# Column maximum of k in three two-input steps, one subtraction for a pair of heads, and a rounding moved to ScalarE, in a fused linear attention and two-MLP kernel

## The chip, the cores and the metric

The kernel runs on one core of one Trainium2 chip. The metric is the device time of one execution in microseconds (us), lower is better. The kernel before was timed in three runs: 1659.59, 1660.09 and 1670.22 us, with a median of 1660.09 us. One more execution was taken under the hardware profiler; all rows shown in this document come from such profiled executions.

## The reference

```python
q_s = softmax of q over its 64 features          # exp(q - max) / (sum + 1e-9)
k_s = softmax of k over its 576 positions        # exp(k - max over positions) / (sum + 1e-9)
kv  = einsum('bhsd,bhse->bhde', k_s, v)          # one 64x64 matrix for each batch and head
x   = einsum('bhsd,bhde->bhse', q_s, kv)         # 8 batches, 8 heads, 576 positions, 64 features
x   = x as 4608 tokens of 512 features
x   = relu(x @ w_in1)**2 @ w_out1                # 512 -> 2048 -> 512
out = silu(x @ w_in2) @ w_out2                   # 512 -> 2048 -> 512
```

All of it is in single precision; the four weight matrices arrive in double precision and are converted on the chip. The line that the change touches is the softmax of k: the maximum is taken for each of the 64 columns over all 576 positions.

## The kernel before, in words

**Stages.** The work is a stream of products on TensorE (PE) in blocks of 512 tokens. First the attention of batch 0 is computed, then the first MLP of block 0 while the attention of batch 1 is made. Blocks 1 to 8 of the first MLP follow, each in eight turns, one for each pair of 128-row slices of the hidden layer. A turn computes the hidden part with seven products in place of eight (`strassen`, its matmuls all on L602), applies the square of relu (`relu2`), and adds the products with the output weights of the turn before (`out_pair`, matmuls on L188 to L190 in `mm3`). Wherever precision needs it, a float32 value is split into a rounded part and a rest: `split` (L116 to L118) lets ScalarE (ACT) copy the value into a rounded type and VectorE (DVE) subtract that copy from the source. From about 705 us on, no attention is left, and from about 900 us on the second MLP runs.

**Attention.** Batches 1 to 7 are worked off in 28 pairs of heads by a generator, `attention()` (L445). It has four phases for each pair (`phase`, L427): the maxima of k and q and the exponent of q; the subtraction and exponent of k and the norm of q; the product of k and v with the transposition of q; the product with q and its evacuation. The main loop asks for one phase at two places of each turn (the `hook` calls with 1 and 6), so a pair lasts two turns; in two turns of block 1 a further phase is asked for, so the first pairs follow each other faster. Batches 0 and 1 are `natural` (`by_chunk = 2`): they keep k's columns as head, feature. In batches 2 to 7, with 24 pairs, the columns of the exponent tile `k` are stored as feature half, head, feature in the half.

**What the pair does with k.** `load` brings k as tile `kr`, 128 partitions by two heads by five chunks by 64 features. `k_max` (L267) reduces the five chunks to one row for each partition, tile `m`; POOL then takes the maximum over the partitions into `mb` (L279). `k_sub` (L283) subtracts `mb` into `k`, `k_exp` (L299) takes the exponent on ACT, and `kv` (L302) multiplies slices of 32 of its columns with v, including a column of ones which gives the sum. `kv_evac` (L313) divides by that sum and masks (L315, L316, L318, tile `m` again), and splits the result into `kvh` and `kvl`, both on DVE (L329, L330). `x` (L400) multiplies them with q. The tile `m` exists once, so the maxima of the next pair cannot be written there until the rounded parts have been read.

**Order.** Each engine executes its instructions in one fixed order. That order is worked out when the kernel is built, from the order of the code and from the build's own estimates of when each input is ready; it differs from the order of the code, except for instructions pinned by `keep_in_program_order`. All loads and stores are issued from one queue, SP, also in order.

Of the kernel before, what the change touches and what calls it, by code (L numbers as in the profile page):

```python
# [10 lines left out]
F32 = mybir.dt.float32  # L11
# [7 lines left out]
AX = mybir.AxisListType  # L19
PSUM = bass.MemoryType.PSUM  # L20
DRAM = bass.MemoryType.DRAM
P = 128
# [9 lines left out]
def kernel(  # L32
# [13 lines left out]
    nc = tc.nc  # L46
    B, H, S, D = q.shape
# [7 lines left out]
    SC = SM // P  # L55
# [36 lines left out]
    def f32(t):  # L92
        return t.bitcast(F32)
# [22 lines left out]
    def split(hi, lo, src):  # L116
        nc.scalar.copy(hi, src)  # L117
        nc.vector.tensor_sub(lo, src, f32(hi))  # L118
# [83 lines left out]
    class Pair:  # L202
# [63 lines left out]

        def k_max(self):  # L267
            m = self.tile("m", [P, 2, D], F32)
            if self.natural:
                t = self.tile("km", [P, 2, 2, D], F32)  # L270
                nc.vector.tensor_max(t, self.kr[:, :, 0:2], self.kr[:, :, 2:4])
                nc.vector.tensor_max(t[:, :, 0], t[:, :, 0], t[:, :, 1])
                r = nc.vector.tensor_max(m, t[:, :, 0], self.kr[:, :, 4])
            else:
                r = nc.vector.reduce_max(m, self.kr.rearrange("p a c d -> p a d c"), axis=AX.X)  # L275
            if (self.b, self.p) == (1, 0):
                tc.keep_in_program_order(r)
            self.m = self.tile("mb", [P, 2, D], F32)
            nc.gpsimd.partition_all_reduce(  # L279
                self.m.rearrange("p a d -> p (a d)"), m.rearrange("p a d -> p (a d)"), P, bass_isa.ReduceOp.max  # L280
            )

        def k_sub(self):  # L283
            self.k = self.tile("k", [P, SC + 1, 2 * D], F32)
            if self.natural:
                nc.vector.tensor_sub(
                    self.k.rearrange("p c (a d) -> p c a d", a=2),
                    self.kr.rearrange("p a c d -> p c a d"),
                    self.m.rearrange("p (c a) d -> p c a d", c=1).to_broadcast([P, SC + 1, 2, D]),
                )  # L290
                return
            for a in range(2):
                nc.vector.tensor_sub(
                    self.k.rearrange("p c (dh a dl) -> p c dh a dl", dh=2, a=2)[:, :, :, a],
                    self.kr[:, a].rearrange("p c (dh dl) -> p c dh dl", dh=2),
                    self.m[:, a].rearrange("p (c dh dl) -> p c dh dl", c=1, dh=2).to_broadcast([P, SC + 1, 2, 32]),
                )

        def k_exp(self):  # L299
            nc.scalar.activation(self.k, self.k, AF.Exp)  # L300
# [1 line left out]
        def kv(self):  # L302
            self.kvp = self.bank(self.p % 2, "kvp")
            n = D if self.natural else 32
            for c in range(SC + 1):
                for i in range(P // n):
                    r = slice(n * i, n * i + n)
                    nc.tensor.matmul(
                        self.kvp[r, 0:D + 1], self.k[:, c, r], self.v[:, c, i % 2],
                        start=(c == 0), stop=(c == SC), skip_group_check=True,  # L310
                    )

        def kv_evac(self):  # L313
            rec = self.tile("rec", [P, 1], F32)
            nc.vector.tensor_scalar_add(rec, self.kvp[:, D:D + 1], 1e-9)  # L315
            nc.vector.reciprocal(rec, rec)  # L316
            t = self.tile("m" if not self.early else "kvt", [P, 2 * D], F32)
            nc.vector.scalar_tensor_tensor(  # L318
                out=t.rearrange("p (a d) -> p a d", a=2),
                in0=self.kvp[:, 0:D].rearrange("p (a d) -> p a d", a=1).to_broadcast([P, 2, D]), scalar=rec,  # L320
                in1=(mask_n if self.natural else mask_t).rearrange("p (a d) -> p a d", a=2),
                op0=ALU.mult, op1=ALU.mult,
            )
            if self.natural:
                self.kv32 = t
                return
            self.kvh = self.tile("kvh", [P, 2 * D], F32R)
            self.kvl = self.tile("kvl", [P, 2 * D], F32R)
            nc.vector.tensor_copy(self.kvh, t)  # L329
            nc.vector.tensor_sub(self.kvl, t, f32(self.kvh))  # L330

        def swap(self, t, name):
            u = apool.tile([P, S32], F32, tag=name, name=name)
# [383 lines left out]
    for a in range(2):  # L717
        e = slice(D * a, D * a + D)
        nc.gpsimd.memset(mask_n[e, e], 1.0)
        for dh in range(2):  # L720
            r = 64 * dh + 32 * a
# [12 lines left out]
    for i in range(NK + 2):  # L734
        a = early[i] if i < NK else None
        b = early[i - 1] if 1 <= i <= NK else None
        c = early[i - 2] if 2 <= i else None
# [54 lines left out]
    t = 0  # L792
# [143 lines left out]
```

## Time and profile before

| quantity | value |
|---|---|
| median of three runs | 1660.09 us |
| profiled execution, its own time | 1662.81 us |
| its span, first to last instruction | 1661.0 us |
| PE busy | 1610.4 us, 97% |
| DVE busy | 996.2 us, 60% |
| ACT busy | 855.8 us, 52% |
| mean granted TensorE clock | 0.999 |
| first and last start of the maximum of k in batches 2 to 7 (L275) | 145.9 and 681.9 us |

The profile gives, for a group of equal instructions, the line, the engine, the operation, output and inputs with shapes, the count, the busy time in us with the mean in ns, and the idle time just before them with what ended it ("releaser"). A row of the waits reads: who waited, for whom, us in total, number of waits, the longest. A row of the timeline reads: start, duration, engine, line, operation. A window row reads: from and to, length, then busy us of PE, of PE's weight loads, of DVE, ACT and POOL. An engine that is idle without holding up another costs nothing.

### The profile page before, as it was taken

How to read it: one execution, taken by the hardware profiler on the slowest of the kernel's cores; microseconds unless marked ns; L12 is line 12 of the kernel's file. 1: busy time of each engine (PE TensorE's matmuls, PEld its weight loads, DVE VectorE, ACT ScalarE, POOL GpSimd, SP SyncE). 2: the span in 40 equal slices, each digit the busy share in tenths (PEclk: the TensorE clock that was granted, in tenths of full speed). 3: DMA queues.
4: the chain of work that ended last, by engine and by line, in shares of the span. 5: the costliest groups of instructions: out<-in, count | busy, mean ns of one | idle time of the engine just before them, and what ended most of it. 6: DMA issues, size and time to landing. Idle time of an engine off the chain costs nothing.

```text
span 1661.0 us, 24854 instructions
## 1 busy us (share of the span) xinstructions
PE 1610.4 (97%) x9624; PEld 1396.8 (84%) x9624; DVE 996.2 (60%) x1695; ACT 855.8 (52%) x1505; POOL 54.4 (3%) x150
## 2 busy tenths in 40 slices
PE   4999999999999999999999999999999999999999
PEld 3566888888888888889998889898988989999897
DVE  7999896886868687642436675345344344444333
ACT  4876675666666565654546554334334334334332
POOL 2000000000001000000000000000000000000000
PEclk9999999999999999999999999999999999999999
DMA  7776767678685776745346864543543543544621
GB/s 207 258 226 192 234 208 255 200 218 240 183 259 156 231 206 221 227 168 199 137 171 244 335 248 161 187 184 123 189 174 128 193 165 134 196 156 148 221 96 39
DMA packets 193510, 320.40 MB, mean 193 GB/s; under 512 B 113264, under 2 KB 142960, under 8 KB 188528
## 3 DMA queue, kind: packets, MB, share of 16 engines
q1 hardware_dynamic: 193392, 318.81, 57.6%
q8 instruction: 76, 1.25, 0.3%
q14 instruction: 42, 0.34, 0.1%
HBM read 248.51 MB, written 70.25 MB: 192 GB/s over the span
## 4 chain that ended last, share of the span: by engine, by line
PE 75%; DVE 10%; DMA 6%; ACT 5%; issue 2%; POOL 1%; SPq 0%; POOLq 0%; DVEq 0%; ACTq 0%
PE a L602 19%; PE c L602 14%; PE y L189 8%; PE y L190 8%; PE y L188 8%; PE op L189 5%; PE op L188 5%; PE op L190 5%; DMA raw<-in_moe_w_in_dram 3%; PE hp L655 2%; DMA raw<-in_moe_w_out_dram 2%; DVE g L118 1%; ACT raw L142 1%; DVE m L275 1%; DVE u L150 1%
## 5 line engine op out<-in xcount | busy, mean ns | idle before, releaser
L602 PE MATMUL a<-x,wah 128*128 128x256 f32 (+1 forms) x1792 | 397.7, 309 | 10.7 <-ACT h L636 6.4
L602 PEld LDWEIGHTS a<-x,wah 128*128 128x128 f32 x1792 | 313.4, 189 | 55.9 <-ACT h L636 11.7
L602 PE MATMUL c<-x,wah 128*128 128x256 f32 (+1 forms) x1344 | 293.4, 305 | 0.2 <-DVE h L623 0.2
L602 PE MATMUL a<-x,wal 128*128 128x256 f32 (+1 forms) x896 | 275.4, 307 | 0.0
L189 PE MATMUL op<-g,w 128*128 128x512 f32 x576 | 229.3, 398 | 3.1 <-DVE g L118 3.1
L188 PE MATMUL op<-g,w 128*128 128x512 f32 x576 | 229.2, 402 | 3.0 <-ACT g L117 3.0
L190 PE MATMUL y<-wb,g 128*128 128x512 f32 x576 | 227.8, 396 | 0.0
L189 PE MATMUL y<-wb,g 128*128 128x512 f32 x576 | 227.4, 395 | 0.0
L602 PEld LDWEIGHTS c<-x,wah 128*128 128x128 f32 x1344 | 225.0, 190 | 1.7 <-DVE h L623 0.6
L190 PE MATMUL op<-g,w 128*128 128x512 f32 x576 | 225.5, 391 | 0.0
L188 PE MATMUL y<-wb,g 128*128 128x512 f32 x576 | 223.2, 389 | 0.4 <-ACT wb L117 0.4
L602 PE MATMUL c<-x,wal 128*128 128x256 f32 (+1 forms) x672 | 204.8, 305 | 0.0
L872 ACT ACTIVATE z<-h 128x768 f32<-128x768 f32 x96 | 81.3, 847 | 226.9 <-DVE h L631 225.7
L602 PEld LDWEIGHTS a<-x,wal 128*128 128x128 f32 x896 | 168.9, 189 | 0.2
L623 DVE TENSOR_TENSOR h<-c,h 128x256 f32<-128x256 f32 (+1 forms) x112 | 53.7, 480 | 190.7 <-PE c L602 189.2
L644 ACT ACTIVATE h<-h 128x512 f32<-128x512 f32 x128 | 80.8, 632 | 105.1 <-DVE h L631 103.7
L118 DVE TENSOR_TENSOR g<-h,g 128x512 fp32r<-128x512 f32 x128 | 88.0, 688 | 77.7 <-ACT g L117 77.4
L118 DVE TENSOR_TENSOR g<-z,g 128x768 fp32r<-128x768 f32 x96 | 91.9, 957 | 67.3 <-ACT g L117 66.9
L627 DVE TENSOR_TENSOR h<-a,h 128x256 f32<-128x256 f32 (+1 forms) x112 | 53.5, 477 | 127.9 <-PE a L602 127.9
L620 ACT COPY h<-a 128x256 f32<-128x256 f32 (+1 forms) x112 | 47.1, 420 | 159.2 <-PE a L602 159.2
L190 PEld LDWEIGHTS op<-g,w 128*128 128x128 f32 x576 | 108.9, 189 | 23.7
L602 PEld LDWEIGHTS c<-x,wal 128*128 128x128 f32 x672 | 127.6, 190 | 0.0
(150 smaller groups left out, 2323.3 us busy)
## 6 DMA issues: line engine op xcount, KB each, us to landing
wah<-wad SPq DMA_DIRECT2D x72, 896.0 KB, 6.5
wal<-wad SPq DMA_DIRECT2D x72, 896.0 KB, 6.0
wb<-wbd SPq DMA_DIRECT2D x30, 1024.0 KB, 4.9
raw<-in_moe_w_in_dram SPq DMA_DIRECT2D x32, 512.0 KB, 5.3
raw<-in_moe_w_out_dram SPq DMA_DIRECT2D x32, 512.0 KB, 5.3
wad<-wah SPq DMA_DIRECT2D x16, 896.0 KB, 4.1
wad<-wal SPq DMA_DIRECT2D x16, 896.0 KB, 5.0
x1d<-o SPq DMA_DIRECT2D x18, 512.0 KB, 5.2
```

What stands on the lines that cost most here:

```text
L118: nc.vector.tensor_sub(lo, src, f32(hi))
L142: first = nc.scalar.activation(f32(lo32), lo32, AF.Copy, scale=2.0 ** -51, bias=2.0)
L188: nc.tensor.matmul(ps, lh, rh, start=first, stop=False)
L189: nc.tensor.matmul(ps, lh, rl, start=False, stop=False)
L190: nc.tensor.matmul(ps, ll, rh, start=False, stop=last)
L602: nc.tensor.matmul(ps, l, r, start=first and c == 0 and n == 0, stop=c == 1 and n == 2, skip_group_check=True)
L620: nc.scalar.copy(h[:, 0, two], a)
L623: nc.vector.tensor_add(h[:, 0, two], c, h[:, 0, two])
L627: nc.vector.tensor_add(h[:, 1, two], a, h[:, 1, two])
L644: nc.scalar.activation(h, src, AF.Relu)
L655: nc.tensor.matmul(hp, f32(w[:, s]), XR[0][:, c], start=c == 0, stop=c == NK - 1)
L872: nc.scalar.activation(z, h, AF.Sigmoid)
```

## The change

In batches 2 to 7 the maximum over the five chunks is no longer one reduction, but three maxima of two inputs, as batches 0 and 1 already have; the subtraction is one instruction for both heads instead of one for each, with k's columns in the order head, feature; the matmuls of `kv` pick their 32 columns from that order, and write the same rows; and the rounded part `kvh` is made by `split`, so by ACT instead of DVE. Batches 0 and 1 execute the same instructions as before.

```diff
         def k_max(self):
             m = self.tile("m", [P, 2, D], F32)
-            if self.natural:
-                t = self.tile("km", [P, 2, 2, D], F32)
-                nc.vector.tensor_max(t, self.kr[:, :, 0:2], self.kr[:, :, 2:4])
-                nc.vector.tensor_max(t[:, :, 0], t[:, :, 0], t[:, :, 1])
-                r = nc.vector.tensor_max(m, t[:, :, 0], self.kr[:, :, 4])
-            else:
-                r = nc.vector.reduce_max(m, self.kr.rearrange("p a c d -> p a d c"), axis=AX.X)
+            t = self.tile("km", [P, 2, 2, D], F32)
+            nc.vector.tensor_max(t, self.kr[:, :, 0:2], self.kr[:, :, 2:4])
+            nc.vector.tensor_max(t[:, :, 0], t[:, :, 0], t[:, :, 1])
+            r = nc.vector.tensor_max(m, t[:, :, 0], self.kr[:, :, 4])
...
         def k_sub(self):
             self.k = self.tile("k", [P, SC + 1, 2 * D], F32)
-            if self.natural:
-                nc.vector.tensor_sub(
-                    self.k.rearrange("p c (a d) -> p c a d", a=2),
-                    self.kr.rearrange("p a c d -> p c a d"),
-                    self.m.rearrange("p (c a) d -> p c a d", c=1).to_broadcast([P, SC + 1, 2, D]),
-                )
-                return
-            for a in range(2):
-                nc.vector.tensor_sub(
-                    self.k.rearrange("p c (dh a dl) -> p c dh a dl", dh=2, a=2)[:, :, :, a],
-                    self.kr[:, a].rearrange("p c (dh dl) -> p c dh dl", dh=2),
-                    self.m[:, a].rearrange("p (c dh dl) -> p c dh dl", c=1, dh=2).to_broadcast([P, SC + 1, 2, 32]),
-                )
+            nc.vector.tensor_sub(
+                self.k.rearrange("p c (a d) -> p c a d", a=2),
+                self.kr.rearrange("p a c d -> p c a d"),
+                self.m.rearrange("p (c a) d -> p c a d", c=1).to_broadcast([P, SC + 1, 2, D]),
+            )
...
             n = D if self.natural else 32
             for c in range(SC + 1):
                 for i in range(P // n):
-                    r = slice(n * i, n * i + n)
+                    at = D * (i % 2) + n * (i // 2)
                     nc.tensor.matmul(
-                        self.kvp[r, 0:D + 1], self.k[:, c, r], self.v[:, c, i % 2],
+                        self.kvp[n * i:n * i + n, 0:D + 1], self.k[:, c, at:at + n], self.v[:, c, i % 2],
...
             self.kvh = self.tile("kvh", [P, 2 * D], F32R)
             self.kvl = self.tile("kvl", [P, 2 * D], F32R)
-            nc.vector.tensor_copy(self.kvh, t)
-            nc.vector.tensor_sub(self.kvl, t, f32(self.kvh))
+            split(self.kvh, self.kvl, t)
```

The helper that it now calls, unchanged:

```python
    def split(hi, lo, src):
        nc.scalar.copy(hi, src)
        nc.vector.tensor_sub(lo, src, f32(hi))
```

## The prediction

> **What bounds the kernel now.** I read the page first, for which engine has no slack.
>
> ```profile
> span 1661.0 us, 24854 instructions
> PE 1610.4 (97%) x9624; PEld 1396.8 (84%) x9624; DVE 996.2 (60%) x1695; ACT 855.8 (52%) x1505; POOL 54.4 (3%) x150
> ```
>
> PE is busy for 97% of the span; a DVE at 60% is no bound on average. All edits lie in the stretch where batches 2 to 7 are made, so the next view is busy time by stretch: the first five pairs, the other nineteen, and the stretch behind the last pair.
>
> ```profile
> 145.00:245.00 100.00, 95.41 (x745) 80.90 (x744) 91.37 (x184) 67.56 (x129) 6.49 (x19) 1.00 0.70 219
> 245.00:705.00 460.00, 446.13 (x3413) 389.62 (x3412) 340.81 (x711) 291.67 (x571) 31.21 (x75) 1.00 0.71 218
> 705.00:900.00 195.00, 194.30 (x1205) 174.65 (x1204) 82.84 (x140) 107.81 (x210) 0.00 (x0) 1.00 0.49 173
> ```
>
> The columns after the length are busy us of PE, PE's weight loads, DVE, ACT and POOL. In the first 100 us DVE is busy 91.4 us, and PE is idle for 100 - 95.41 = 4.6 us. In the next 460 us DVE has 460 - 340.8 = 119 us to spare, and PE is idle for 13.9 us. Behind the attention PE is idle for 0.7 us of 195. So whatever the edits free on DVE, the end can come earlier by at most about 4.6 + 13.9 = 18.5 us. Which part of that do the touched instructions cause? The waits of PE, first from 145 to 245, then from 245 to 705:
>
> ```profile
> PE op L189 <- DVE g L118: 3.1, 5, 1.4
> PE a L602 <- ACT h L636: 0.7, 2, 0.5
> PE op L188 <- ACT g L117: 0.6, 1, 0.6
> ...
> PE xp L188 <- DVE kvh L329: 5.4, 9, 1.6
> PE a L602 <- ACT h L636: 5.1, 9, 1.7
> PE a L602 <- ACT h L620: 2.2, 4, 0.6
> PE a L602 <- DVE h L627: 0.8, 1, 0.8
> ```
>
> The first group, 4.4 us, is a full DVE that delivers the hidden values late. Of the second group only the first row names a touched instruction: nine times in nineteen pairs PE stands 0.6 us for the rounded part kvh. The third, four waits, comes where one block passes to the next; its chain is shown further down.
>
> **The change part by part.** These are the rows for the old forms, and for the new ones, which batch 1 already runs:
>
> ```profile
> L275 DVE TENSOR_REDUCE m<-kr 128x128 f32<-128x640 f32 x24 | 31.7, 1319 | 0.5
> L293 DVE TENSOR_TENSOR k<-kr,mb 128x320 f32<-128x320 f32 x48 | 21.8, 487 | 11.2 <-POOL mb L279 11.2
> L329 DVE CAST kvh<-m 128x128 fp32r<-128x128 f32 x24 | 5.3, 221 | 0.2
> L286 DVE TENSOR_TENSOR k<-kr,mb 128x640 f32<-128x640 f32 x4 | 3.3, 818 | 1.4 <-POOL mb L279 1.4
> L342 DVE TENSOR_REDUCE qm<-q 128x10 f32<-128x640 f32 x4 | 3.3, 815 | 0.0
> L271 DVE TENSOR_TENSOR km<-kr 128x256 f32<-128x256 f32 x4 | 1.7, 416 | 0.0
> L272 DVE TENSOR_TENSOR km<-km 128x128 f32<-128x128 f32 x4 | 1.2, 288 | 0.0
> L273 DVE TENSOR_TENSOR m<-km,kr 128x128 f32<-128x128 f32 x4 | 1.1, 287 | 0.0
> ```
>
> *Maximum.* 1319 ns go, 416 + 288 + 287 = 991 ns come: 0.33 us less on DVE for each pair by durations. What they take on the engine depends on their neighbours:
>
> ```profile
> 44.04 0.42 DVE L271 TENSOR_TENSOR km<-kr 128x256 f32<-128x256 f32 x1
> ...
> 44.81 0.29 DVE L273 TENSOR_TENSOR m<-km,kr 128x128 f32<-128x128 f32 x1
> ...
> 115.17 0.28 DVE L272 TENSOR_TENSOR km<-km 128x128 f32<-128x128 f32 x1
> 115.37 0.81 DVE L342 TENSOR_REDUCE qm<-q 128x10 f32<-128x640 f32 x1
> ...
> 118.57 0.28 DVE L273 TENSOR_TENSOR m<-km,kr 128x128 f32<-128x128 f32 x1
> 118.77 0.69 DVE L149 TENSOR_SCALAR w<-w 128x1024 uint32<-128x1024 uint32 x1
> ```
>
> Back to back, each step waits for the one before: 44.04 to 45.10, 1.06 us, so 0.26 us less than 1.32. Spread among other work, each small step holds DVE for only 0.20 us (115.17 to 115.37), the first for some 0.33 (0.42 less the same overlap): 0.73 us, against about 1.24 for the reduction by that overlap, so 0.51 us less. Bounds 0.26 to 0.51 us. The second fence shows something else: the build spreads the three steps apart. Only the third writes tile m, which the pair before must have released; the first two need only kr, and can run earlier. Thus behind the release stand 0.29 us instead of 1.32.
>
> *A rule against this edit.* The Trainium skill, page "VectorE: DVE Perf Modes", section "Rules for kernel authors", says of chained operations to minimize their count; its section on the TRN2 errata gives a two-input float32 operation (N + 151) / 0.96 ns, so 424 + 291 + 291 = 1006 ns for the three, and 824 ns for one pass over 640 elements. By that, estimated from the page, this edit would cost DVE 0.18 us for each pair, and the sum below would be about -1.7. The trace agrees on the two-input steps and on L342 (815), but L275 takes 1319 for as many elements; it steps over 64 elements between neighbours. The row decides; the case stands among the rivals.
>
> *Subtraction.* From the chain that ended last, at the passage from one block to the next (start, us, what):
>
> ```profile
> 342.72 1.33 DVE m L275
> ...
> 345.24 0.90 DVE k L293 x2
> ...
> 347.95 0.67 ACT qh L117
> 348.63 0.28 ACT h L620
> ```
>
> Two subtractions of 487 ns, which hold DVE for 0.90 us together, become one of 818 ns: 0.08 us less. One semaphore release fewer; nothing hangs on the first half, since the exponent takes both.
>
> *Columns of k.* The matmuls keep their number and shapes. Their four slices of 32 columns began at 0, 32, 64, 96 and begin at 0, 64, 32, 96 now, so no slice is new, and the exponent runs over the tile as a whole: 0, from both sides.
>
> *Rounding.* 221 ns leave DVE. ACT has no row of this shape. Its casts give the slope:
>
> ```profile
> L117 ACT CAST g<-h 128x512 fp32r<-128x512 f32 x128 | 79.5, 622 | 2.8
> L117 ACT CAST wah<-c 128x1792 fp32r<-128x1792 f32 x16 | 27.0, 1690 | 8.0 <-DVE c L499 5.1 <-issue 2.8
> L422 ACT COPY xe<-xp 128x64 f32<-128x64 f32 x28 | 6.3, 227 | 0.0
> ```
>
> (1690 - 622) / 1280 = 0.83 ns for an element and 195 ns fixed: 302 ns for 128, between 227 (64 elements) and 622 (512) in any case. ACT is 63% busy from 245 to 705, so 24 times 0.3 us = 7.2 us of work fit; what matters is the place in its queue. One of the nine waits of PE:
>
> ```profile
> 272.15 0.62 ACT L117 CAST g<-h 128x512 fp32r<-128x512 f32 x1
> 272.51 0.34 DVE L318 SCALAR_TENSOR_TENSOR m<-kvp,rec,mask_t 128x128 f32<-128x128 f32 x1
> 272.68 0.37 ACT L613 COPY h<-a 128x256 f32<-128x256 f32 x1
> 272.81 0.69 DVE L118 TENSOR_TENSOR g<-h,g 128x512 fp32r<-128x512 f32 x1
> 272.94 0.38 ACT L616 COPY h<-c 128x256 f32<-128x256 f32 x1
> 273.42 0.22 DVE L329 CAST kvh<-m 128x128 fp32r<-128x128 f32 x1
> 273.79 0.37 PE L188 MATMUL xp<-qh,kvh 128*128 128x288 f32 x1 [0.54 <-DVE kvh L329]
> ```
>
> The masked product ends at 272.85, and the rounding waits on DVE until 273.42 behind another block's subtraction; it ends at 273.64. On ACT it could run from 272.85 or 273.05 (after L613) and end at 273.15 to 273.35; behind L616, from 273.32, it ends at 273.62. That is a gain of 0.02 to 0.49 us; I take 0.25 (the middle), times nine = 2.2 us. Bounds: nothing, and the whole 5.4.
>
> *The new waits.* ACT now stops for DVE's masked product, and behind it in its queue stand L613, L616 and the casts of the hidden values, for which PE and DVE wait. kvl on DVE now waits for ACT, and behind it the third maximum and the splits. In the other fifteen pairs PE does not wait today; if each did as the nine do (0.6 us), that is 15 x 0.54 = 8.1 us as an upper bound, 0 the lower. I take 1.2, two of the fifteen, because L613 and L616 read banks which PE needs again only after further output products (the rows above have none waiting for them).
>
> *Where DVE is full.* For each pair DVE is relieved by 0.26 + 0.08 + 0.22 = 0.56 up to 0.51 + 0.08 + 0.22 = 0.81 us: 13 to 19 us over 24 pairs, most of it beside idle DVE time. From 145 to 245 it counts: five pairs, 2.8 to 4.0 us, against 4.4 us of waits. Part of each such chain is not DVE; I take 2.0, bounds 0 and 4.4. At the passage of blocks the chain shown above runs through the touched lines L275 and L293 to the copy L620, for which PE then waits 2.2 / 4 = 0.55 us. 0.34 us at least leave this chain (0.26 + 0.08), more if the first two steps move up into time that is free. I take 0.37 x 4 = 1.5, bounds 0 and 2.2. Late next is nothing that the trace shows there. The 5.1 us for L636 follow converted weights, which no edit touches: 0. SP also gains: kr is released earlier by its shorter maximum and subtraction, so loads queue a little earlier; I count 0.
>
> **Sum:** -2.0 - 2.2 - 1.5 + 1.2 = -4.5 us. On the profiled execution: 1662.8 - 4.5 = 1658.3 (its span 1661.0, with 1.8 us around it, becomes 1656.5). That execution lies 2.7 us above the median of the runs, 1660.1; in terms of that median I forecast **1655.6**.
>
> **The rivals.** *No gain:* DVE's relief falls into its 119 idle us, the order is worked out anew, and waits only change places: 1660.1. For it speaks that nineteen of the 24 pairs lie in the stretch with idle DVE; against it, that the rows name kvh itself. *All of it:* the waits of the first group and those for kvh and L620 all go: 4.4 + 5.4 + 2.2 = 12.0, so 1648.1. Against it: ACT needs its own 0.3 us and has a queue. *Slower:* the rounding now stands in ACT's queue, behind casts of 0.62 us. It decides where ACT comes free more than about 0.3 us later than DVE would have. Then PE waits for kvh in all 24 pairs at today's mean: 24 x 0.6 = 14.4 in place of 5.4, so +9.0; less 3.5 for the full DVE, +5.5: 1665.6. For it: ACT's casts and copies run without a gap around 272 to 273.3. Against it: DVE has such a queue today, and kvh stands behind 0.69 us there. *Three steps dearer than one:* if the reduction took what L342 takes for 640 elements, 815 ns, three steps of 991 would add 0.18 us, and a pair would be relieved by 0.08 + 0.22 - 0.18 = 0.12 us instead of 0.56; the two terms of the full DVE shrink to a fifth, -0.4 and -0.3, and with -2.2 + 1.2 the sum is -1.7: 1658.4. L275's own 1319 speaks against it. This is the skill's rule of the count, named above.
>
> **How the numbers follow.** Forecast 0.45, no gain 0.22, dearer steps 0.03, slower 0.20, all of it 0.10. The forecast's own range is 1652 to 1659. The range of 1648 to 1667 reaches to both outer cases with 1.4 us beyond the slower one, because its bound of 15 waits could be met with a dearer one, and one run in three of the kernel before was 10 us above the others. A measurement of this kernel can tell about 1% from no change, 16.6 us: faster means under 1643.5, which needs nearly all 18.5 us of idle PE and is left 0.03; slower means over 1676.7, three times the slower rival, 0.04; the rest is 0.93.
>
> **What would show it.** Right: 28 instances each of the three steps on tiles km and m, at 0.42, 0.29 and 0.29 us; one subtraction of 0.82 for a pair; a cast kvh on ACT near 0.30; DVE's busy time down by about 15 us (996 to 981) and ACT's up by 7; PE's wait for kvh down from 5.4 us to about 3, its waits for g (L118) from 145 to 245 from 3.1 to near 1, for L620 from 2.2 to under 1. Wrong: PE's waits for kvh above 7 us, or new rows with ACT waiting for the masked product followed by PE waiting for L613, L616 or L636; idle PE between 145 and 705 at 18 us or more with DVE relieved as worked out, which would mean no gain.

## The result and the profile after

Compared on one chip, the kernel before takes 1662.99 us (median of 8 runs, 1655.51 to 1670.22), the changed one 1653.45 us (median of 8 runs, 1651.33 to 1655.97). The ratio is 0.9943, with a 95% interval of 0.9927 to 0.9959: 9.5 us faster, between 6.8 and 12.1. That is inside the range of 1648 to 1667 us, of the predicted sign, and twice the predicted size of 4.5 us. The differences in us, here and for the experiments, are worked out from the ratio and not from the two medians, which can give another figure (6.8 us where the ratio of `e4_max_sub` gives 9.6). The ratios leave out two slow executions, one of `e4_max_sub` (2645.15 us) and one of the kernel before (5603.08 us).

The profiled execution of the changed kernel took 1653.48 us, 9.3 less than that of before. First the head of its page, then busy time in the first two of the prediction's stretches (length; busy us of PE, PE's weight loads, DVE, ACT, POOL). Line numbers behind `k_max` are smaller by up to 12 than before: L270 to L272 are the three steps, L282 the subtraction, L590 the matmuls that were L602, L608 the copy that was L620, L624 the one that was L636.

```profile
span 1651.7 us, 24836 instructions
PE 1607.9 (97%) x9624; PEld 1397.8 (85%) x9624; DVE 982.1 (59%) x1695; ACT 858.1 (52%) x1529; POOL 50.6 (3%) x150
```

```profile
145.00:245.00 100.00, 98.22 (x770) 84.33 (x769) 88.65 (x190) 70.51 (x142) 7.71 (x21) 1.00 0.70 222
245.00:705.00 460.00, 451.55 (x3457) 397.34 (x3456) 333.36 (x711) 297.17 (x596) 27.11 (x72) 1.00 0.72 219
```

In the first 100 us PE is now idle for 1.8 us instead of 4.6, in the next 460 for 8.5 instead of 13.9: 8.2 us less in all. DVE's busy time fell by 14.1 us, as worked out (996 to 982 against a forecast of 981). ACT's rose by 2.3 us (855.8 to 858.1) and not by the 7 that were forecast, although the new casts alone are busy for 7.1. The new instructions have the durations that were taken for them:

```profile
L282 DVE TENSOR_TENSOR k<-kr,mb 128x640 f32<-128x640 f32 x28 | 23.0, 822 | 13.4 <-POOL mb L276 13.4
L270 DVE TENSOR_TENSOR km<-kr 128x256 f32<-128x256 f32 x28 | 11.7, 419 | 8.3 <-DMA kr<-in_k_dram 8.3
L271 DVE TENSOR_TENSOR km<-km 128x128 f32<-128x128 f32 x28 | 8.0, 286 | 0.5
L272 DVE TENSOR_TENSOR m<-km,kr 128x128 f32<-128x128 f32 x28 | 8.0, 286 | 0.4
L117 ACT CAST kvh<-m 128x128 fp32r<-128x128 f32 x24 | 7.1, 296 | 1.6 <-DVE m L307 1.6
```

The first step now runs so early that it waits for k's load, 8.3 us of DVE's spare time in all. PE's waits from 140 to 705, complete:

```profile
PE xp L188 <- ACT kvh L117: 4.8, 7, 1.5
PE a L590 <- ACT h L624: 1.8, 4, 1.1
PE op L189 <- DVE g L118: 1.1, 3, 0.5
PE xp L190 <- DVE kvl L118: 1.0, 3, 0.3
PE xp L188 <- DVE qmu L323: 0.8, 2, 0.4
```

These 9.5 us stand against some 18 before. The row for kvh has hardly shrunk (5.4 before). What shrank is the waits for hidden values: g L118 from 3.1 to 1.1, the copy at the end of a turn (L636, now L624) from 0.7 + 5.1 to 1.8, and the copy L620, now L608, from 2.2 to no row.

Not all of a difference between two profiled executions is the change's. The last matmul of block 0 on the hidden layer, ahead of the stretch that the change touches, starts at 144.1 us before and at 143.1 after (the sixth figure of the row is the last start):

```profile
L655 PE MATMUL hp<-xr,w x128: 590/592/697, 31.6 to 144.1; 128*128 128x512 f32 x128
```

```profile
L643 PE MATMUL hp<-xr,w x128: 590/592/697, 31.0 to 143.1; 128*128 128x512 f32 x128
```

Over all executions profiled here that start lies between 141.0 and 144.1, and both ends belong to kernels whose orders up to there are exactly the same (`e11_halves` and the kernel before). So a single pair of profiles can be off by 2 us and more, and the verdicts below rest on the ratios of many runs. In this pair of profiles some of the lead is given back behind the attention. The row of PE's waits for the same sum of hidden values, before from 705 to 930 and after from 695 to 920:

```profile
PE a L602 <- DVE h L627: 0.4, 1, 0.4
```

```profile
PE a L590 <- DVE h L615: 2.1, 2, 1.1
```

### The profile page after: what moved, and what is told of

It reads as the page before. It is cut to its first block, busy times and chain, and to the rows that moved or that the text cites. A ratio compares the mean times of both kernels' runs of the same rounds, so it can differ in the third digit from the quotient of the medians.

```text
span 1651.7 us, 24836 instructions
## 1 busy us (share of the span) xinstructions
PE 1607.9 (97%) x9624; PEld 1397.8 (85%) x9624; DVE 982.1 (59%) x1695; ACT 858.1 (52%) x1529; POOL 50.6 (3%) x150
## 4 chain that ended last, share of the span: by engine, by line
PE 58%; DMA 3%; ACT 2%; DVE 1%; issue 0%; SPq 0%; ACTq 0%; DVEq 0%
PE a L590 16%; PE c L590 11%; PE y L189 8%; PE y L190 8%; PE y L188 8%; PE op L189 2%; PE op L190 2%; PE op L188 2%; DMA raw<-in_moe_w_out_dram 1%; DMA c<-wf 1%; DMA x1d<-o 1%; DMA raw<-in_moe_w_in_dram 0%; ACT h L633 0%; ACT h L632 0%; ACT raw L142 0%
## 5 line engine op out<-in xcount | busy, mean ns | idle before, releaser
L590 PE MATMUL a<-x,wah 128*128 128x256 f32 (+1 forms) x1792 | 396.0, 308 | 6.1 <-ACT h L624 2.6
L590 PEld LDWEIGHTS a<-x,wah 128*128 128x128 f32 x1792 | 314.1, 189 | 48.2 <-ACT h L624 5.5
L590 PE MATMUL c<-x,wah 128*128 128x256 f32 (+1 forms) x1344 | 293.5, 305 | 0.0
L590 PE MATMUL a<-x,wal 128*128 128x256 f32 (+1 forms) x896 | 275.5, 307 | 0.0
L590 PEld LDWEIGHTS c<-x,wah 128*128 128x128 f32 x1344 | 225.2, 190 | 0.9 <-DVE h L611 0.2
L590 PE MATMUL c<-x,wal 128*128 128x256 f32 (+1 forms) x672 | 204.8, 305 | 0.0
L590 PEld LDWEIGHTS a<-x,wal 128*128 128x128 f32 x896 | 169.0, 189 | 0.2 <-DVE wal L118 0.2
L118 DVE TENSOR_TENSOR g<-h,g 128x512 fp32r<-128x512 f32 x128 | 88.1, 688 | 76.6 <-ACT g L117 76.0
L118 DVE TENSOR_TENSOR g<-z,g 128x768 fp32r<-128x768 f32 x96 | 91.8, 956 | 67.4 <-ACT g L117 66.9
L608 ACT COPY h<-a 128x256 f32<-128x256 f32 (+1 forms) x112 | 46.7, 417 | 156.8 <-PE a L590 156.6
L590 PEld LDWEIGHTS c<-x,wal 128*128 128x128 f32 x672 | 127.6, 190 | 0.0
```

Of the source, the lines that this page charges most:

```text
L590: nc.tensor.matmul(ps, l, r, start=first and c == 0 and n == 0, stop=c == 1 and n == 2, skip_group_check=True)
L608: nc.scalar.copy(h[:, 0, two], a)
```

## The experiments

Every experiment starts from the kernel before and was timed against it in five rounds. The theories, under the names that the expectations use: **one**, the gain follows the VectorE time freed; **two**, in the first four runs the place of the rounding, in `e5_together` to `e7_payback` the early release (two steps run before tile m is free); **three**, the build's order comes out differently by chance; **four**, time that the order does not reckon with, because the build takes the reduction for as short as a contiguous one; **five**, the length of one uninterrupted instruction that stands ahead of others.

**The three parts, one at a time.** The edits are those of the change's diff. `e1_max` has the three-step maximum, `e2_sub` the subtraction and the columns, `e3_round` the rounding, `e4_max_sub` the maximum and the subtraction.

> The kernel before with the three-step maximum alone. Theory one, time of VectorE: the gain of the whole change, 9.5 us, follows the VectorE time that it frees, 0.33 + 0.16 + 0.22 us for each pair; this part frees 0.33, so about -4.5 us (1658.5 if the kernel before stands at 1663). Theory two, the place of the rounding: the gain is that kvh no longer stands in VectorE's queue, so this part gives -1 us at most. Theory three, the order: what counts is the order that the build works out anew, and the result has no relation to the time freed: anything from -9 to +5.

Measured: 1654.67 against 1662.57 us, ratio 0.9954 (0.9938 to 0.9970), -7.6 us.

> The kernel before with the single subtraction and k's columns in order alone. Theory one: frees 0.16 us of VectorE for each pair by durations (0.08 by start to start), so -1 to -2 us. Theory two: 0. Theory three: by more than 3 us either way, although hardly any time is freed.

Measured: 1662.64 us, ratio 1.0004 (0.9991 to 1.0017), +0.7 us.

> The kernel before with the rounding of kvh moved to ScalarE alone. Theory one: frees 0.22 us for each pair on VectorE, so -3 us. Theory two: nearly the whole gain, -7 to -9 us. Theory three: no relation; slower than before would speak for it.

Measured: 1663.55 us, ratio 1.0001 (0.9988 to 1.0014), +0.2 us. PE waits for the rounded part as it did, now for ACT. Its row in this kernel, to be read against 5.4 us and nine waits before:

```profile
PE xp L188 <- ACT kvh L117: 3.8, 8, 1.2
```

> The change without the rounding on ScalarE: three-step maximum and single subtraction. Theory one: 0.49 of 0.71 us freed, so -6 to -7 us, and the sum of the first two kernels of this call. Theory two: -1 us at most. Theory three: not the sum of the two parts.

Measured: 1655.73 us, ratio 0.9942 (0.9920 to 0.9964), -9.6 us.

What follows: the maximum carries the gain. The other two parts by themselves are within 2 to 3 us of nothing. The rounding's place (theory two of these runs) is out. `e2_sub` and `e3_round` laid the order out anew as well and changed nothing, which speaks against chance in the order (theory three) but does not exclude it; `e9_contig`, further down, does, since it has the gain in an unchanged order. Theory one stands so far, since the maximum frees most time, but its size was off already: it expected 4.5 us of `e1_max`, and the interval runs from 5.0 to 10.3.

**Release or time.** `e5_together` writes all three steps in tile m, so none may run before its release; `e6_free_m` gives the single reduction a tile that is free:

```diff
-            m = self.tile("m", [P, 2, D], F32)
+            m = self.tile("m", [P, 2, D], F32) if self.natural else None
...
-                r = nc.vector.reduce_max(m, self.kr.rearrange("p a c d -> p a d c"), axis=AX.X)
+                t = self.tile("m", [P, 2, 2, D], F32).rearrange("p c a d -> p a c d")
+                nc.vector.tensor_max(t, self.kr[:, :, 0:2], self.kr[:, :, 2:4])
+                nc.vector.tensor_max(t[:, :, 0], t[:, :, 0], t[:, :, 1])
+                m = t[:, :, 0]
+                r = nc.vector.tensor_max(m, m, self.kr[:, :, 4])
```

```diff
-            m = self.tile("m", [P, 2, D], F32)
+            m = self.tile("m" if self.natural else "km", [P, 2, D], F32)
```

> The kernel before with the three-step maximum, but all three steps write in tile m, so none can run before the pair before has released it. VectorE's time is that of the three-step maximum. Theory one, VectorE's time: as the three-step maximum alone, -5 to -8 us. Theory two, the release: the gain comes from two of three steps running ahead of the release, so it is gone here: 0 to -2 us.

Measured: 1655.78 against 1664.85 us, ratio 0.9947 (0.9935 to 0.9959), -8.8 us.

> The kernel before with its single reduction, but written into the tile that batch 1 uses for its intermediate maxima and that lies unused after it, so it needs not wait until the pair before has released tile m. VectorE's time is unchanged. Theory one, VectorE's time: 0, within 2 us. Theory two, the release: -5 to -8 us.

Measured: 1663.86 us, ratio 0.9996 (0.9983 to 1.0010), -0.7 us. The reduction did run ahead, as its idle time shows: it waits for k's load now.

```profile
L275 DVE TENSOR_REDUCE km<-kr x24: 1246/1310/1348, 133.6 to 673.6; 128x128 f32<-128x640 f32 x24
its engine sat idle before it (us, times) until:
  DMA kr<-in_k_dram: 12.0, 11
```

The gain stays without the early release, so the release is not what brings it. In `e6_free_m` it did not bring the gain either; there the orders of PE and ACT came out differently too, so that run by itself shows less.

**Giving the time back.** `e7_payback` has the three-step maximum and executes its first step twice in batches 2 to 7 (the doubled line is a copy of the first `tensor_max`).

> The three-step maximum alone, with its first step executed twice in batches 2 to 7, which gives 0.33 to 0.42 us of VectorE's time back for each pair: about what the edit freed. Theory one, VectorE's time: the gain is gone, 0 to -2 us. Theory two, the release: the doubled step also runs ahead of the release, so the gain stays, -5 to -8 us.

Measured: 1656.99 us, ratio 0.9953 (0.9939 to 0.9967), -7.8 us. Both copies take their time, so the maximum costs 0.42 + 0.42 + 0.29 + 0.29 = 1.42 us of DVE for each pair, more than the reduction's 1.32:

```profile
L271 DVE TENSOR_TENSOR km<-kr x28: 403/418/427, 43.2 to 663.8; 128x256 f32<-128x256 f32 x28
```

```profile
L273 DVE TENSOR_TENSOR km<-kr x24: 407/424/428, 135.1 to 664.3; 128x256 f32<-128x256 f32 x24
```

Theory one falls: the time is back, and the gain stays. One could object that the second copy falls into idle VectorE time (its neighbour waits for k's load) and so is not paid where VectorE is full. The window from 145 to 245 us of this kernel, to be read against the prediction's row for the kernel before, says no: VectorE is busy for 92.3 us there, before for 91.4, and PE is idle for 1.1 us instead of 4.6 (single profiles).

```profile
145.00:245.00 100.00, 98.87 (x776) 85.16 (x775) 92.33 (x208) 69.91 (x138) 7.53 (x22) 1.00 0.73 227
```

**Where.** `e8_first2` uses the three steps only for the first two of the 24 pairs (`if self.natural or (self.b, self.p) in ((2, 0), (2, 1))`).

> The three-step maximum in the first two pairs of batch 2 alone, the reduction in the other 22. If the gain arises where VectorE is full, in the first turns of block 1 (the turns' ends of the three-step kernel lead by 3.7 us there, its lead up to that stage deducted): -3 to -4 us. If each pair adds its share: 2/24 of -7.6, -0.6 us.

Measured: 1660.81 us, ratio 0.9980 (0.9970 to 0.9990), -3.3 us. So two pairs in the first turns of block 1 bring some two fifths of what all 24 bring (3.3 of 7.6, the 3.3 with an interval of 1.7 to 5.0); the rest is left for the other 22 pairs.

**What it is about the reduction.** `e9_contig` leaves every order as it is and only makes the reduction shorter, by letting it take its maxima over five neighbouring values in place of the five chunks; `e10_slow` leaves every order as in `e1_max` and makes the three steps longer; `e11_halves` cuts the reduction in two; `e12_overpay` adds a longer instruction.

```diff
-                r = nc.vector.reduce_max(m, self.kr.rearrange("p a c d -> p a d c"), axis=AX.X)
+                r = nc.vector.reduce_max(m, self.kr.rearrange("p a c d -> p a (c d)").rearrange("p a (d c) -> p a d c", c=SC + 1), axis=AX.X)
```

```diff
+            x, z = ((lambda y: y),) * 2 if self.natural else (lambda y: y.rearrange("p a c d -> p a d c"), lambda y: y.rearrange("p a d -> p d a"))
...
-                nc.vector.tensor_max(t, self.kr[:, :, 0:2], self.kr[:, :, 2:4])
+            nc.vector.tensor_max(x(t), x(self.kr[:, :, 0:2]), x(self.kr[:, :, 2:4]))
...
```

```diff
-                r = nc.vector.reduce_max(m, self.kr.rearrange("p a c d -> p a d c"), axis=AX.X)
+                for a in range(2):
+                    r = nc.vector.reduce_max(m[:, a], self.kr[:, a].rearrange("p c d -> p d c"), axis=AX.X)
```

```diff
+                if not self.natural:
+                    nc.vector.tensor_max(self.kr, self.kr, self.kr)
                 nc.vector.tensor_max(t, self.kr[:, :, 0:2], self.kr[:, :, 2:4])
```

> The kernel before, its orders on all engines instruction for instruction the same, but the single reduction reads neighbouring elements (it takes its maxima over five neighbouring values of a partition instead of over the five chunks; this part of the computation is changed). L342 suggests 0.82 us for it instead of 1.32. Theory four, time that the order does not reckon with: the build lays out the order as if the reduction took as long as a contiguous one, so 0.5 us of each pair come unplanned; without them -6 to -9 us. Theory one, VectorE's time: also -6 to -9. Theory five, the length of one instruction that holds up the others: a third of the gain, -2 to -3.

Measured: 1655.62 against 1663.24 us, ratio 0.9950 (0.9931 to 0.9969), -8.3 us. The reduction's row:

```profile
L275 DVE TENSOR_REDUCE m<-kr x24: 777/813/821, 144.7 to 675.9; 128x128 f32<-128x640 f32 x24
```

> The three-step maximum alone, its orders on all engines the same as in the kernel with that part alone, but each step walks its tiles with the stride innermost, which the build does not reckon with; if that costs 0.8 ns for an element as in the reduction, the steps take 0.4 us more, 1.4 in all. Theory four: the time is unplanned again, the gain is gone, 0 to -2 us. Theory one: gone as well, but then the doubled step should have lost it too. Theory five: three short instructions still, the gain stays, -5 to -8.

Measured: 1657.67 us, ratio 0.9957 (0.9941 to 0.9972), -7.2 us, though the steps are as long as meant, 0.63 + 0.39 + 0.39 = 1.41 us (medians; four of the 28 are batch 1's and short):

```profile
L271 DVE TENSOR_TENSOR km<-kr x28: 403/626/648, 43.0 to 667.9; 128x256 f32<-128x256 f32 x28
```

```profile
L272 DVE TENSOR_TENSOR km<-km x28: 282/393/403, 43.5 to 668.6; 128x128 f32<-128x128 f32 x28
```

Theory four expected the gain to go, since the order does not reckon with the added 0.4 us; it stays. What the run leaves of theory four is a weaker form, since here the 0.4 us come in pieces of 0.1 and 0.2 us, and in the reduction 0.5 us come in one piece.

> The kernel before with the reduction split into one for each head: two instructions of about 0.75 us in place of one of 1.32. Theory five, the length of one instruction: -3 to -6 us. Theory four: their 0.25 us each stay unplanned, 0 within 2 us. Theory one: 0 to +2.

Measured: 1660.67 us, ratio 0.9980 (0.9969 to 0.9991), -3.3 us, with no less VectorE time: two of 730 ns.

```profile
L276 DVE TENSOR_REDUCE m<-kr 128x64 f32<-128x320 f32 x48 | 33.3, 730 | 0.6
```

The edit did not do all that it was meant to, though. In 21 of the 24 pairs the two halves stand directly behind each other on VectorE and hold it for about 1.38 us, as the whole reduction did; one such pair:

```profile
196.41 1.35 DVE L276 TENSOR_REDUCE m<-kr 128x64 f32<-128x320 f32 x2
```

Only the second, third and seventh pair have other work between the halves, the first two of them where VectorE is full. That two pairs in that stretch bring 3.3 us in `e8_first2` as well fits this.

> The three-step maximum alone with one more instruction ahead of it in batches 2 to 7, the maximum of tile kr with itself, 0.82 us that the build reckons with: VectorE then works 0.5 us longer for each pair than in the kernel before. Theory four: most of the gain stays, -4 to -8 us. Theory one: slower than before, +2 to +8 us. Theory five: 0.82 us in one piece costs a part of the gain, -2 to -5.

Measured: 1656.62 us, ratio 0.9962 (0.9948 to 0.9975), -6.3 us, while the maximum takes 1.81 us of DVE for each pair:

```profile
L272 DVE TENSOR_TENSOR kr<-kr 128x640 f32<-128x640 f32 x24 | 19.7, 820 | 12.8 <-DMA kr<-in_k_dram 12.8
```

Put together, by VectorE time of the maximum in a pair and by its longest single instruction (both in us, sums and medians from the rows above and from the prediction's):

| kernel | time in a pair | longest instruction | ratio |
|---|---|---|---|
| before | 1.32 | 1.32 | 1 |
| e6_free_m | 1.31 | 1.31 | 0.9996 |
| e11_halves | 1.46 | 0.73, twice | 0.9980 |
| e12_overpay | 1.81 | 0.82 | 0.9962 |
| e9_contig | 0.81 | 0.81 | 0.9950 |
| e10_slow | 1.41 | 0.63 | 0.9957 |
| e7_payback | 1.42 | 0.42 | 0.9953 |
| e1_max | 0.99 | 0.42 | 0.9954 |
| e5_together | 0.99 | 0.42 | 0.9947 |

The column of times does not order the ratios: 1.81 gains 6.3 us, 1.31 gains nothing. The column of the longest instruction nearly does: above 1.3 us no gain, at 0.82 and below most or all of it. Only the halves stand out, and they stand back to back in 21 pairs. Two comparisons are the sharpest, because no order differs in them: `e9_contig` takes 0.5 us from the one long instruction and has the gain, while `e10_slow` adds 0.4 us to the three short ones of `e1_max` and loses nothing that can be measured.

Theory five is the one that fits best, but it is not shown. It had expected a third of the gain of `e9_contig` (2 to 3 us; measured 8.3, interval 5.2 to 11.5) and at most 5 us of `e12_overpay` (measured 6.3, interval 4.2 to 8.6). And if neighbouring pieces are counted as one, the order of the column is lost: the three steps of `e5_together` stand back to back in 11 pairs, for about 1.13 us, with a gain of 8.8 us. Theory four in its weaker form, 0.5 us in one piece with which the order does not reckon, fits the table as well: this time is in the kernel before, in `e6_free_m` and, back to back, in most pairs of `e11_halves`, and in no kernel with the whole gain. The timeline of DVE at the second pair shows how either would act. Before, the subtraction of the hidden values stands behind the whole reduction, and PE waits 0.30 us for it:

```profile
161.75 0.29 DVE L330 TENSOR_TENSOR kvl<-m,kvh 128x128 fp32r<-128x128 f32 x1
...
162.14 1.33 DVE L275 TENSOR_REDUCE m<-kr 128x128 f32<-128x640 f32 x1
163.39 1.48 DVE L118 TENSOR_TENSOR g<-h,g 128x512 fp32r<-128x512 f32 x2
...
164.12 0.50 PE L189 MATMUL op<-g,w 128*128 128x512 f32 x1 [0.30 <-DVE g L118]
```

In `e9_contig` the same instructions follow each other in the same order, and PE has no such wait there:

```profile
160.35 0.82 DVE L275 TENSOR_REDUCE m<-kr 128x128 f32<-128x640 f32 x1
161.09 1.49 DVE L118 TENSOR_TENSOR g<-h,g 128x512 fp32r<-128x512 f32 x2
```

With three steps (`e1_max`) each waits for the one before it, and the two subtractions of hidden values stand in between:

```profile
157.13 0.28 DVE L272 TENSOR_TENSOR km<-km 128x128 f32<-128x128 f32 x1
...
158.13 0.68 DVE L118 TENSOR_TENSOR g<-h,g 128x512 fp32r<-128x512 f32 x1
158.73 0.28 DVE L330 TENSOR_TENSOR kvl<-m,kvh 128x128 fp32r<-128x128 f32 x1
159.06 0.69 DVE L118 TENSOR_TENSOR g<-h,g 128x512 fp32r<-128x512 f32 x1
159.67 0.29 DVE L273 TENSOR_TENSOR m<-km,kr 128x128 f32<-128x128 f32 x1
```

From kvl to the start of the first such subtraction it is 163.39 - 161.75 = 1.64 us before; here, in another order, that subtraction starts 0.60 us ahead of kvl.

**What stays open.** The runs show that it is the form of the maximum, and neither its total time nor its early release. Whether the length of one instruction is the cause, or the 0.5 us in one piece with which the order does not reckon, they do not show: a long instruction with whose whole length the order reckons, put in the reduction's place, was not tried. Nor were the waits of the other 22 pairs traced one by one, and the runs cannot separate the whole change (0.9943) from the maximum alone (0.9954).

## Why the prediction was right, and where it was off

**What bounds the kernel.** Right: the gain stayed under the 18.5 us of idle PE, and in the pair of profiles 8.2 us came out of that idle time in the two stretches named.

**Durations.** Right within 2%: 419, 286, 286 and 822 ns against 416, 288, 287 and 818, and 296 ns for the rounding on ACT against 302 estimated from the slope of its casts. DVE's relief came out as worked out.

**The rivals.** "No gain", "slower" and "three steps dearer than one" lie outside the interval. The measured 9.5 us lie between the forecast of 4.5 and "all of it", 12.0, and nearer to the latter, which had a chance of 0.10; but that rival let the waits for kvh go, and those stayed. The forecast's own range, 1652 to 1659, is a gain of 1.1 to 8.1 us and does not hold 9.5. That the measured 1653.45 us look close to the forecast 1655.6 is luck: the kernel before stood 2.9 us higher in this comparison than in the three runs from which the forecast was counted.

**Rounding, -2.2, and its new waits, +1.2.** Together -1.0; alone the part measured +0.2 with an interval of 2 us either way, which does not exclude it. The row, though, shows that the first half was too hopeful: PE's wait for kvh went from 5.4 to 4.8 us in the changed kernel, not to 3. The waits that I allowed for came: 1.0 us for kvl, a row that was not there before. (The upper bound for them, 8.1 us, takes 0.54 us where the sentence says 0.6; it would be 9.0, and no term of the sum rests on it.)

**Where DVE is full, -2.0.** The place was right, the size rather too small: PE's idle time there fell by 2.8 us, and the first two pairs alone bring 3.3 us (1.7 to 5.0) with the maximum only.

**The passage of blocks, -1.5.** The place was right, and the gain there is the upper bound: the row for L620, 2.2 us, is gone from 140 to 705 in the changed kernel.

**L636, counted as 0.** These waits shrank without having been counted: 5.8 us before, 1.8 after, in single profiles. I had put the 5.1 us behind 245 us down to the converted weights alone. The trace before bears this out for three of the nine waits, 3.9 us, in which the copy stands in ACT's queue behind L145, a step of the conversion; ahead of the other six, 0.2 us each, ACT had itself waited 1.4 to 2.1 us for VectorE. But this row does not explain the missing 5 us: in `e1_max`, which brings 7.6 us, it is 4.6 us, and in `e12_overpay`, which brings 6.3, it is 6.6.

```profile
PE a L602 <- ACT h L636: 4.6, 6, 1.3
```

```profile
PE a L602 <- ACT h L636: 6.6, 10, 2.4
```

So which waits shrink differs between kernels with nearly the same gain, and from which of them the missing 5 us come stays open.

**The step that failed** is the measure by which the gain was counted: "For each pair DVE is relieved by 0.26 + 0.08 + 0.22 = 0.56 up to 0.51 + 0.08 + 0.22 = 0.81 us", with the gain read from that sum where DVE is full. The time freed was right, and it is not what paid: `e7_payback` and `e12_overpay` give all that the maximum freed back and keep the gain or most of it, while the subtraction and the rounding, which together free about half of it, each bring nothing that can be measured. The prediction saw that the three steps are spread by the build, and drew from it only that two of them can run before tile m is released; `e5_together` and `e6_free_m` show that this is not the point.

**The rule weighed.** The advice of the Trainium skill to minimize the count of chained operations ("VectorE: DVE Perf Modes", section "Rules for kernel authors") would have spoken against the part that brought the gain. Another page of the Trainium skill, "Perfetto Trace Analysis", section "Optimizing Scalar/DVE Operations", says that where such an engine is not saturated and yet causes gaps on others, breaking up instructions may let work end sooner. The runs agree: four instructions of together 1.42 us beat one of 1.32 by 7.8 us.

## What to carry to other kernels

On an engine that runs in a fixed order and serves a busier one, look for its longest single instruction among those for which the busier engine does not wait directly, and ask what stands behind it; here, cutting it into dependent pieces paid even where the pieces took longer in all. Cutting alone is not enough: see in the trace whether other work comes between the pieces. Test a gain from freed time by giving the time back in small pieces, and see that it is given back where the engine is full: if the gain stays, it was not the time. Where one part of a change of three carries all of it, only runs of the parts can tell, since the profile after shows all three as worked out.

## What the runs showed of the hardware

A stride of 64 elements between neighbours costs VectorE about 0.8 ns for each element here. A reduction of 640 elements takes 1319 ns with it (the kernel before) and 813 ns when they are adjacent (`e9_contig`), 506 / 640 = 0.79 ns; a maximum of two inputs over 256 elements takes 418 ns plain and 626 ns with the stride innermost (`e10_slow`), 208 / 256 = 0.81 ns, and over 128 elements 286 and 393 ns, 0.84 ns. The Trainium skill, "SBUF — State Buffer", section "Door 1: The DMA port swizzle (why `[64,N]` ≈ `[32,N]`)", says that accesses which cross to a new 16-byte line pay a penalty, so that four float32 values are free; it gives no price, and these rows agree with it in kind.
